# One score tile in twenty of a stage exponentiated on VectorE, in a two-layer transformer kernel; narrow units transposed on TensorE; half-width buffers for tanh-GELU

## The chip, the cores and the metric

The kernel runs on one core of a Trainium2 chip. A core has a matrix engine (TensorE, PE in the profile; its weight loads are PEld), a vector engine (VectorE, DVE), an activation engine (ScalarE, ACT), a general engine (GpSimd, POOL) and a queue that issues transfers (SyncE, SP). They run at the same time, each through its own list of instructions in a fixed order, and wait for each other by semaphores. The metric is the device time of one launch in microseconds (us). Four runs of the kernel before took 1085.89, 1086.05, 1086.89 and 1088.29 us, a median of 1086.47.

## The reference

The input is 2048 rows of 448 numbers in bf16. Two identical layers are applied, each an attention block (A) with 16 heads of 28 and a mixer with an MLP (B):

```python
def _A_ref(x, wqkv, wo):
    B, S, D = x.shape
    H = 16
    Dh = D // H
    qkv = (lambda x, *d: x.transpose(*d))((x @ wqkv).reshape(B, S, 3, H, Dh), 2, 0, 3, 1, 4)
    q, k, v = qkv[0], qkv[1], qkv[2]
    scores = jnp.einsum("bhqd,bhkd->bhqk", q, k) * (Dh ** -0.5)
    p = _softmax(scores, axis=-1)
    o = jnp.einsum("bhqk,bhkd->bhqd", p, v)
    return (lambda x, *d: x.transpose(*d))(o, 0, 2, 1, 3).reshape(B, S, D) @ wo

def _B_ref(x, w1, w2, w3, w4):
    ...
    h = _gelu(_layernorm(x, axis=-1) @ w1)
    ...
    hs = jnp.concatenate([g0, g1, g2, g3], axis=-1) @ w2
    x1 = x + hs
    h2 = _gelu(_layernorm(x1, axis=-1) @ w3) @ w4
    return x1 + h2

x = A_x
x = x + _A_ref(_layernorm(x, axis=-1), A_wqkv, A_wo)
x = x + _B_ref(_layernorm(x, axis=-1), B_w1, B_w2, B_w3, B_w4)
x = x + _A_ref(_layernorm(x, axis=-1), A_wqkv, A_wo)
x = x + _B_ref(_layernorm(x, axis=-1), B_w1, B_w2, B_w3, B_w4)
```

Here g0 to g3 are four column blocks of h, shifted by one or two rows up or down, and gelu is the tanh form.

## The kernel before, in words

**Tiles.** The 2048 rows are 16 tiles of 128. Queries are worked in units of four tiles (512 queries); in the second layer (the code's L = 1) the last four tiles are two narrow units of two tiles. The heads are four groups of four, g = 0 to 3, each head padded from 28 to 32 rows, so that four heads fill the 128 rows of the array. The "middle query units" of the first layer (the code's L = 0) are units 1 and 2.

**Attention.** A segment is one unit, one group of heads and a range of key tiles (all 16, or a part for the units that start before all keys exist; a part's unfinished sum is spilled to DRAM from `u_sb` and loaded again into `uin`). Within a segment, every pair of a key tile and a head is a score tile: 128 keys by 512 queries, one PSUM bank. Score tiles are gathered in granules of three and two by turns, 823 granules for 2048 score tiles. Granule n uses banks 0 to 2 or 3 and 4 (`gbank`). For each, PE computes the scores (`st_ops`), ACT exponentiates the whole granule in one instruction into `PT`, which holds six granules, and PE multiplies it with the values into bank 5 (`t_pv`). The scores of granule n+2 are asked for when the exponentiation of n has been placed, since they use the same banks. At the end of a segment `t_norm` takes the sum out of bank 5, adds the earlier part, and divides by the row of sums. There is no running maximum: a bound, taken from norms of queries and keys, rides along as an extra row of `qT` and keeps the exponent in range.

**The rest.** `kq_proj`, `k_proj`, `q_proj` and `v_proj` make keys, queries and values; `t_outproj` the output projection; `t_mixA` the norm and the matmul with w1, whose gelu `tanh_gelu` computes on VectorE with one tanh on ACT; `t_x1` the matmul with w2 and the second norm; `t_mixB` the MLP, with its hidden rows in `h2T`. `t_gelu` applies the MLP's gelu in batches, since each needs another function table on ACT. Units of one tile at the very end work `direct`: ACT applies gelu as it reads PSUM, and the normalized rows are transposed on PE instead of by a DMA (`transposes`, `pe_transpose`).

**What sets the order.** All this is written as small tasks, generators that yield operations with an estimated duration, the keys they read and write, waits for named events and requests for named resources (banks, buffers). At build time the scheduler `Sched` places one operation after another on the engine lists, by the earliest start and by a rank. It plans twice, each time taking the latest starts of the last plan as the due times of the next, and the final round perturbs the due times at given clock values with given random seeds (`MOVES`). So an edit of one task can move instructions of all the others. Semaphores follow from the keys. While PE would idle, the scheduler places filler matmuls on `ones_bf` into a free bank (the line of the profile with `ones_bf` and 128x256). A lone matmul of four column blocks may be cut into four narrow ones beside the attention products (`cols4`), which is why one operation has two lines in the profile.

Lines of the profile that the prediction uses: L1183 exponentiation; L1157 scores; L1207 products with the values; L1223, L1225 and L1229 the end of a segment; L1294 to L1302 `tanh_gelu`; L1511 batched gelu; L643 and L646 other matmuls, whole and in four; L1547 filler; L909 and L914 the copies of queries and keys on ACT; L918 `sq`; L1473 the copies of the MLP's hidden rows out of PSUM.

Of the kernel before, what the change touches and what calls it, by code (L numbers as in the profile page):

```python
# [496 lines left out]
def build_kernel(nc, A_x, A_wqkv, A_wo, B_x, B_w1, B_w2, B_w3, B_w4, out, n_layers=2):  # L497
# [9 lines left out]
    WSH = 60.0 / SCALE  # L507
# [6 lines left out]
            (0.00, 729633), (12.02, 924040), (24.04, 434439), (36.20, 574974), (48.20, 998734), (60.31, 612851), (84.52, 842410), (96.68, 918064),  # L514
            (108.85, 164590), (120.87, 267692), (157.65, 500181), (169.69, 831239), (181.82, 304948), (230.86, 623460), (267.82, 635046), (279.92, 554061),
            (291.98, 583939), (316.31, 70253), (354.68, 913365), (427.30, 772407), (439.37, 109773), (451.37, 312812), (463.53, 356989), (499.73, 313895),
            (511.74, 819503), (523.90, 509392), (536.08, 765633), (560.47, 911140), (572.67, 320651), (584.70, 124158), (596.84, 268927), (608.90, 282420),
            (623.07, 286925), (647.19, 306544), (671.29, 953155), (683.47, 435091), (720.44, 443516), (732.70, 487532), (744.73, 525952), (756.74, 580821),
            (780.78, 167669), (804.93, 534508), (817.06, 491945), (829.27, 156654), (841.43, 565799), (865.63, 783778), (883.33, 193326), (907.37, 77659),
            (919.44, 633974), (931.74, 778092), (955.90, 220356), (967.93, 984671), (979.95, 491738), (1004.15, 124983), (1016.21, 872429), (1029.60, 388275),  # L520
            (1041.62, 163375), (1053.71, 7157),
# [15 lines left out]
        [([0, 1, 2], 0, 0), ([3, 4, 5, 6], 4, 0), ([7, 8, 9, 10], 0, 1), ([11, 12], 4, 2), ([13, 14, 15], 0, 2)],  # L537
        [([0, 1, 2], 4, 0), ([3, 4, 5, 6], 0, 0), ([7, 8, 9, 10], 4, 1), ([11, 12], 0, 1), ([13], 2, None), ([14, 15], 4, None)],
# [28 lines left out]
    with st:  # L567
# [7 lines left out]
        hot = sb("hot", [128, 4], FP32)  # L575
        ident = sb("ident", [128, 128], BF16)
# [7 lines left out]
        h2T = sb("h2T", [128, 14, 1024], BF16)  # L584
# [32 lines left out]
        PT = sb("PT", [128, 15, 512], BF16)  # L617
        u_sb = sb("u_sb", [128, 512], FP32)
# [478 lines left out]
        def e_dur(n):  # L1097
            return 0.066 + 0.427 * len(grans[n]) if n >= 0 else 0.0
# [18 lines left out]
        def t_uload(si):  # L1117
            L, u, g, p, kts, first, last = segs[si]
            yield ("wait", ("spill", L, u, p - 1, g))
            if not segs[si - 1][5]:  # L1120
                yield ("wait", ("ucopied", si - 1))
# [515 lines left out]
```

## Time and profile before

| | |
|---|---|
| median of four runs | 1086.47 us |
| the profiled execution | 1087.08 us |
| its span, first to last instruction | 1085.4 us |
| PE busy, filler included | 1047.0 us |
| ACT busy | 1036.4 us |
| DVE busy | 597.0 us |
| POOL busy | 54.1 us |
| mean granted TensorE clock | 0.995 |
| moved by DMA | 38.33 MB |

A line of the groups names the line of the code, the engine, the operation, what it writes and reads, the number of instructions, then their busy time in us and the mean of one in ns, and last how long the engine stood idle before them and which instruction ended most of that. Windows give each engine's busy time in a stretch of the span. Durations of neighbouring instructions on one engine can overlap a little, so their sum is somewhat more than the time they take together. Busy time of PE is modelled from pipelined matmuls.

### The profile page before, as it was taken

Reading aid. Unit: us, or ns where it says so; the run is one execution under the profiler, and the core shown is the slowest. Engines: PE = TensorE matmul, PEld = TensorE weight load, DVE = VectorE, ACT = ScalarE, POOL = GpSimd, SP = SyncE. Lnnn points to the kernel's source line nnn. Section 1 sums busy time; section 2 is a strip of 40 time slices with the busy share of each in tenths; the row PEclk is TensorE's granted clock in tenths of the full one; section 3 lists DMA queues with packets and bytes.
Section 4 is the critical chain, followed back from the end, with each engine's and each line's share of the span. In section 5 each row is a group of like instructions: output and inputs, shape, how many; then the busy total and the mean of one; then the engine's idle time right before and its main releaser. Section 6 shows DMA issues by size and latency. Waiting matters only on the chain.

```text
span 1085.4 us, 21565 instructions
## 1 busy us (share of the span) xinstructions
PE 1047.0 (96%) x9390; PEld 409.7 (38%) x9408; DVE 597.0 (55%) x1410; ACT 1036.4 (95%) x938; POOL 54.1 (5%) x76
## 2 busy tenths in 40 slices
PE   8999999999999999999999999999999999999998
PEld 5333333333333432334333333333333333444545
DVE  6976248420573356832688438356957323757434
ACT  4899999999999999999999999999999999999973
POOL 1100000000010000100001000000000000010000
PEclk8999999999999999999999999999999999999999
DMA  4222080000000020000111112214200001000000
GB/s 113 59 84 64 20 193 21 15 1 21 20 21 2 1 40 21 1 21 1 40 40 33 31 31 59 69 30 118 54 20 2 21 10 32 22 21 12 11 18 22
DMA packets 76439, 38.33 MB, mean 35 GB/s; under 512 B 61176, under 2 KB 69752, under 8 KB 76344
## 3 DMA queue, kind: packets, MB, share of 16 engines
q1 hardware_dynamic: 76344, 36.96, 13.3%
q8 instruction: 73, 1.20, 0.5%
q14 instruction: 22, 0.18, 0.1%
HBM read 13.75 MB, written 8.13 MB: 20 GB/s over the span
## 4 chain that ended last, share of the span: by engine, by line
ACT 60%; PE 34%; DVE 5%; DMA 1%; issue 0%; SPq 0%; DVEq 0%; ACTq 0%
ACT PT L1183 53%; PE ps L643 12%; PE ps L1157 8%; PE ps L1207 7%; ACT h2T L1511 4%; PE ps L646 4%; PE ps L1547 2%; ACT gt L1299 1%; DMA xT<-xn 1%; ACT L1511 1%; DMA h2T<-in_A_wqkv_dram 1%; ACT L1183 0%; DVE kT L911 0%; DVE st L805 0%; DVE hT L1290 0%
## 5 line engine op out<-in xcount | busy, mean ns | idle before, releaser
L1183 ACT ACTIVATE PT<-ps 128x1536 bf16<-128x1536 f32 (+1 forms) x823 | 938.3, 1246 | 8.0 <-PE ps L1157 5.4
L1157 PE MATMUL ps<-qT,kT 32*128 32x512 bf16 (+1 forms) x2304 | 320.0, 360 | 14.3 <-ACT PT L1183 7.9
L1207 PE MATMUL ps<-PT,vaug 128*32 128x512 bf16 (+1 forms) x2304 | 249.8, 362 | 3.3 <-ACT PT L1183 1.4
L1547 PE MATMUL ps<-ones_bf 128*128 128x256 bf16 x1234 | 185.5, 278 | 2.6 <-DVE hot L677 1.1
L1157 PEld LDWEIGHTS ps<-qT,kT 32*128 32x128 bf16 x2304 | 80.3, 91 | 264.1 <-ACT PT L1183 155.4
L1473 DVE CAST h2T<-ps 128x512 bf16<-128x512 f32 (+2 forms) x126 | 73.8, 586 | 111.5 <-PE ps L643 88.7
L1547 PEld LDWEIGHTS ps<-ones_bf 128*128 128x128 bf16 x1234 | 102.7, 99 | 85.7 <-issue 62.8
L643 PE MATMUL ps<-xT,w 112*128 112x512 bf16 (+6 forms) x632 | 127.8, 323 | 0.8 <-ACT h2T L1470 0.4
L1207 PEld LDWEIGHTS ps<-PT,vaug 128*32 128x32 bf16 x2304 | 63.4, 94 | 124.1 <-issue 69.3
L643 PEld LDWEIGHTS ps<-xT,w 112*128 112x128 bf16 (+1 forms) x632 | 50.5, 104 | 52.6 <-issue 29.6
L643 PE MATMUL ps<-w,h2T 128*128 128x448 bf16 x259 | 62.2, 362 | 4.0 <-ACT h2T L1511 4.0
L646 PE MATMUL ps<-w,h2T 128*32 128x448 bf16 x756 | 48.7, 353 | 4.4 <-ACT h2T L1511 4.4
L1229 DVE SCALAR_TENSOR_TENSOR u_sb<-uin,fct,ps 128x512 f32<-128x512 f32 x24 | 17.8, 743 | 59.1 <-PE ps L1207 58.0
L646 PE MATMUL ps<-xT,w 112*32 112x512 bf16 (+3 forms) x576 | 48.8, 349 | 0.1
L1490 DVE TENSOR_TENSOR uin<-x_res,ps 128x448 bf16<-128x448 bf16 x16 | 9.8, 619 | 66.1 <-PE ps L643 49.8
L1497 DVE TENSOR_TENSOR x_res<-x_res,ps 128x448 bf16<-128x448 bf16 x16 | 9.9, 620 | 64.3 <-PE ps L646 35.3
L1511 ACT ACTIVATE h2T<-h2T 128x7168 bf16<-128x7168 bf16 (+2 forms) x9 | 44.7, 5008 | 0.1
L805 DVE BATCH_NORM_STATS2 st<-x_res 128x6 f32<-128x448 bf16 x64 | 38.9, 615 | 1.7 <-DMA x_res<-in_A_x_dram 0.9
L1334 POOL TENSOR_TENSOR mst<-mst,neghalf 128x4 f32<-128x4 f32 (+2 forms) x10 | 9.0, 895 | 535.8 <-DVE mst L1333 407.9
L911 DVE TENSOR_SCALAR qT<-ps,bcol 128x512 bf16<-128x512 f32 (+1 forms) x24 | 15.6, 650 | 36.4 <-PE ps L643 35.3
L1432 POOL TENSOR_TENSOR mst<-mst,neghalf 128x1 f32<-128x1 f32 x32 | 22.7, 718 | 255.1 <-DVE mst L1430 218.6
L1223 DVE STREAM_TRANSPOSE u_sb<-ps 128x512 f32<-128x512 f32 (+1 forms) x24 | 15.0, 624 | 34.5 <-PE ps L1207 34.5
(139 smaller groups left out, 901.9 us busy)
## 6 DMA issues: line engine op xcount, KB each, us to landing
uscr<-u_sb SPq DMA_DIRECT2D x24, 256.0 KB, 2.1
uin<-uscr SPq DMA_DIRECT2D x24, 256.0 KB, 2.7
w<-in_B_w_dram SPq DMA_DIRECT2D x2, 1568.0 KB, 14.3
out_dram<-uin SPq DMA_DIRECT2D x16, 112.0 KB, 1.7
x_res<-in_A_x_dram SPq DMA_DIRECT2D x3, 448.0 KB, 8.8
h2T<-in_A_wqkv_dram SPq DMA_DIRECT2D x2, 392.0 KB, 6.0
w<-in_B_w_dram SPq DMA_DIRECT2D x2, 392.0 KB, 8.4
xT<-xn SPq DMA_TRANSPOSE x32, 3.7
```

Source lines behind the costliest of these rows:

```text
L643: return e.matmul(out=dst(0, m), lhsT=lhs(0, m), rhs=rhs, start=start, stop=stop)
L646: return [e.matmul(out=dst(a, min(m, a + 32)), lhsT=lhs(a, min(m, a + 32)), rhs=rhs, start=start, stop=stop, tile_position=(0, a)) for a i ...
L805: yield op("dve", 0.55, lambda e: e.bn_stats(out=st6[:, t, :], in_=x_res[:, t, :]), reads=[("x", t)], writes=[("st6", t)])
L911: yield op("dve", 0.06 + c_ps(nw), lambda e, b=b: e.tensor_scalar(out=dst, in0=ps[:, bi(b), 0:nw], scalar1=bias, scalar2=None, op0=ALU.add ...
L1157: yield op("pe", 0.005 if ph == h else 0.012 + W / 2400.0, lambda e, bk=bk, r0=32 * j, g=g, kc=kc, q0=q0, W=W, c0=W * h: e.matmul(out=ps[: ...
L1183: yield op("act", e_dur(n), lambda e, b0=b0, p0=p0, cnt=cnt: e.activation(out=PT[:, p0:p0 + cnt, :], in_=ps[:, b0:b0 + cnt, :], func=ACT.E ...
L1207: yield op("pe", 0.004 + nt * 0.0133, lambda e, j=j, rhs=rhs, vs=vs, i=i: e.matmul(out=ps[32 * j:32 * j + 32, UBK, 0:128 * nt], lhsT=vaug[ ...
L1229: yield op("dve", 0.06 + c_ps(W), lambda e: e.scalar_tensor_tensor(out=u_sb[:, 0:W], in0=uin[:, :], scalar=fct[:, L, p, g:g + 1], in1=ps[: ...
L1432: yield op("pool", 0.57, lambda e, t=t: e.tensor_tensor(out=mst[:, t, R3:R3 + 1], in0=mst[:, t, V3E:V3E + 1], in1=neghalf[:, 0:1], op=ALU. ...
L1473: yield op("dve", c_ps(NW), lambda e, fch=fch, b=b: e.tensor_copy(out=h2T[:, fch, hoff:hoff + NW], in_=ps[:, bi(b), 0:NW]), reads=[("ps", ...
L1511: yield op("act", c_act(14 * NW), lambda e, c0=c0, NW=NW: e.activation(out=h2T[:, :, c0:c0 + NW], in_=h2T[:, :, c0:c0 + NW], func=ACT.Gelu ...
L1547: SC.fill = (0.13, lambda e, b: e.matmul(out=ps[:, bi(b), 0:256], lhsT=ones_bf[:, :], rhs=ones_bf[:, :].unsqueeze(1).to_broadcast([128, 2, ...
```

## The change

One score tile of some granules no longer goes through ACT. `on_dve` picks granules by their number and by the place of their third tile in its segment. For these ACT exponentiates the first two tiles only, and a task `t_dexp` computes the third on VectorE in seven operations: the scores, in units of the exponent of two, are clamped at zero and written as 32-bit integers with 16 fractional bits; from the low half a correction polynomial is made in fp16 (in `gt`, the buffer of the tanh); the sum of the shifted integer and the correction, written as 16-bit integers into a buffer `PTD` of three slots, is the bit pattern of the power of two in bf16. The third score matmul of granule n+2 waits until the first of these operations has read the bank. The products with the values of such a tile are deferred by `DEFER` key tiles in `t_pv`. So that the same scores serve both engines, queries are scaled by `QS` and ACT's exponentiation has scale `LN2` and a constant bias.

Around it: `h2T` has seven tiles instead of eight, with other places in `MIXB`; units of two tiles or fewer are transposed on PE in `t_mixA`, and in the second layer's `t_mixB`; `tanh_gelu` takes halves of its two work buffers where the unit is at most 256 wide; a later part's sum is added in place in `uin` and spilled from there, and the last part's transpose writes `u_sb`; the batched gelu of a narrow tile of the second layer has no margin in its planned start; and `MOVES` is another list.

```diff
-    WSH = 60.0 / SCALE
+    LN2 = math.log(2.0)
+    QS = SCALE / LN2
+    BIAS2 = 127.0
+    WSH = 60.0 / LN2 + BIAS2
+    DEFER = 4
+    EXPC = (0.30457565 * 128, 0.07826797 * 128)
...
-        [([0, 1, 2], 0, 0), ([3, 4, 5, 6], 4, 0), ([7, 8, 9, 10], 0, 1), ([11, 12], 4, 2), ([13, 14, 15], 0, 2)],
-        [([0, 1, 2], 4, 0), ([3, 4, 5, 6], 0, 0), ([7, 8, 9, 10], 4, 1), ([11, 12], 0, 1), ([13], 2, None), ([14, 15], 4, None)],
+        [([0, 1, 2], 0, 0), ([3, 4, 5, 6], 3, 0), ([7, 8, 9, 10], 0, 1), ([11, 12], 4, 2), ([13, 14, 15], 0, 2)],
+        [([0, 1, 2], 4, 0), ([3, 4, 5, 6], 0, 0), ([7, 8, 9, 10], 3, 1), ([11, 12], 0, 1), ([13], 2, None), ([14, 15], 3, None)],
...
+        t32 = sb("t32", [128, 512], mybir.dt.int32)
...
-        h2T = sb("h2T", [128, 14, 1024], BF16)
+        h2T = sb("h2T", [128, 14, 896], BF16)
...
+        PTD = sb("PTD", [128, 3, 512], BF16)
...
-            b2 = yield from kq_proj(xt, g, wq_pad, "wq_pad", qT[:, g, q0:q0 + nw], wk, bias, bkey, nw)
+            b2 = yield from kq_proj(xt, g, wq_pad, "wq_pad", qT[:, g, q0:q0 + nw], wk, bias, bkey, nw, QS)
...
+        def on_dve(n):
+            if len(grans[n]) < 3:
+                return False
+            L, u, g, p, kts, first, last = segs[grans[n][2][0]]
+            return 1 <= grans[n][2][1] <= len(kts) * UNITS[L][u][1] // 4 - 4 and (104 < n < 300 and n % 8 == 0)
+
+        DVL = [n for n in range(len(grans)) if on_dve(n)]
+        DVN = {n: k % 3 for k, n in enumerate(DVL)}
...
+        def t_dexp(n):
+            bk, slot, at = gbank(n) + 2, DVN[n], DVL.index(n)
+            yield ("acq", ["t32"])
+            yield op("dve", 0.06 + c_ps(512), lambda e: e.tensor_scalar(out=t32[:, :], in0=ps[:, bk, :], scalar1=0.0, scalar2=65536.0, op0=ALU.max, op1=ALU.mult),
+                     reads=[("ps", bk)], writes=[("t32",)], last=[("ps", bk)])
+            yield ("sig", ("d1", n))
+            for r in ("gt0", "gt1"):
+                yield ("acq", [r])
+            fx, ex = gt[:, 0:256].bitcast(FP16), gt[:, 256:512].bitcast(FP16)
+            lo = t32[:, :].bitcast(mybir.dt.uint16).rearrange("p (n two) -> p n two", two=2)[:, :, 0]
+            yield op("dve", c_f2b(512), lambda e: e.tensor_scalar(out=fx, in0=lo, scalar1=2.0 ** -16, scalar2=None, op0=ALU.mult), ...
+            yield op("dve", c_b2b(512), lambda e: e.tensor_scalar(out=ex, in0=fx, scalar1=EXPC[1], scalar2=EXPC[0], op0=ALU.mult, op1=ALU.add), ...
+            yield op("dve", c_f2b(512), lambda e: e.tensor_tensor(out=ex, in0=ex, in1=fx, op=ALU.mult), ...
+            yield op("dve", c_b2b(512), lambda e: e.tensor_scalar(out=fx, in0=fx, scalar1=-1.0, scalar2=None, op0=ALU.add), ...
+            yield op("dve", c_f2b(512), lambda e: e.tensor_tensor(out=ex, in0=ex, in1=fx, op=ALU.mult), ...
+            if at >= 3:
+                yield ("wait", ("pvd", DVL[at - 3]))
+            yield op("dve", 0.06 + c_ps(512), lambda e: e.scalar_tensor_tensor(out=PTD[:, slot, :].bitcast(mybir.dt.uint16), in0=t32[:, :], scalar=2.0 ** -9, in1=ex, op0=ALU.mult, op1=ALU.add),
+                     reads=[("t32",), (("gt",), "gt1")], writes=[pt_key(n, 2)])
...
                 for (h, k, si, i, j) in sorted(mms):
+                    if k == 2 and n - 2 in DVN:
+                        yield ("wait", ("d1", n - 2))
...
-                yield op("act", e_dur(n), lambda e, b0=b0, p0=p0, cnt=cnt: e.activation(out=PT[:, p0:p0 + cnt, :], in_=ps[:, b0:b0 + cnt, :], func=ACT.Exp, scale=SCALE),
+                yield op("act", e_dur(n), lambda e, b0=b0, p0=p0, cnt=cnt: e.activation(out=PT[:, p0:p0 + cnt, :], in_=ps[:, b0:b0 + cnt, :], func=ACT.Exp, scale=LN2, bias=-BIAS2 * LN2),
...
+                    now = [h for h in held if h[0] + DEFER <= i * nt // 4]
...
-                yield op("dve", 0.06 + c_ps(W), lambda e: e.scalar_tensor_tensor(out=u_sb[:, 0:W], in0=uin[:, :], scalar=fct[:, L, p, g:g + 1], in1=ps[:, UBK, :],
+                yield op("dve", 0.06 + c_ps(W), lambda e: e.scalar_tensor_tensor(out=uin[:, :], in0=uin[:, :], scalar=fct[:, L, p, g:g + 1], in1=ps[:, UBK, :],
...
+                usrc, uk = (u_sb, ("u",)) if first else (uin, ("uin",))
+                yield op("sp", 0.1, lambda e: e.dma_start(out=uscr[4 * u + g], in_=usrc[:, :]), reads=[uk], writes=[("uscr", u, g)], dma=True, dma_time=3.0)
...
+            if nw <= 256:
+                r = yield ("acq", ["gw0", "gw1"])
+                held = [r]
...
-            yield from transposes(xs, xt, n, direct)
+            yield from transposes(xs, xt, n, direct or n <= 2)
...
-            yield from transposes(xs, xt, n, direct)
+            yield from transposes(xs, xt, n, direct or (L == n_layers - 1 and n <= 2))
...
-                         reads=allk, writes=allk, tab="gelu", margin=0.0 if k else 1.0, glue=k > 0)
+                         reads=allk, writes=allk, tab="gelu", margin=0.0 if k or (L == n_layers - 1 and n <= 2) else 1.0, glue=k > 0)
```

## The prediction

> **What bounds the kernel now.** I read the page first: busy time of the engines and its slices.
>
> ```profile
> PE 1047.0 (96%) x9390; PEld 409.7 (38%) x9408; DVE 597.0 (55%) x1410; ACT 1036.4 (95%) x938; POOL 54.1 (5%) x76
> ...
> DVE  6976248420573356832688438356957323757434
> ACT  4899999999999999999999999999999999999973
> ```
>
> PE and ACT both look full, so a share of busy time does not say which one limits. The groups with shapes kept apart decide it (columns: names, shapes, count, then busy us and mean ns, then idle before and its releaser).
>
> ```profile
> L1183 ACT ACTIVATE PT<-ps 128x1536 bf16<-128x1536 f32 x410 | 599.8, 1463 | 4.2 <-PE ps L1157 2.5 <-PE ps L1207 0.3
> L1183 ACT ACTIVATE PT<-ps 128x1024 bf16<-128x1024 f32 x405 | 420.9, 1039 | 3.8 <-PE ps L1157 2.9 <-PE ps L1207 0.8
> ...
> L1547 PE MATMUL ps<-ones_bf 128*128 128x256 bf16 x1234 | 185.5, 278 | 2.6 <-DVE hot L677 1.1 <-DVE k L1041 1.0 <-ACT qT L909 0.5
> ```
>
> The 823 exponentiations wait for anything only 8.0 us in all (4.2 + 3.8), while 185.5 us of PE is the filler matmul on `ones_bf`, whose result nobody reads. Without it PE is busy 1047.0 - 185.5 = 861.5 us, 79% of the span. ACT is the bound from the first exponentiation to the last; PE has room. The ACT timeline of the stage that the change touches, and then its windows, show it:
>
> ```profile
> 187.50 110.73 ACT L1183 ACTIVATE PT<-ps 128x1536 bf16<-128x1536 f32 x97
> ```
>
> ```profile
> core 0: us, PE busy (x) PEld busy (x) DVE busy (x) ACT busy (x) POOL busy (x), PEclk, DMA share, GB/s
> 160.00:200.00 40.00, 38.73 (x324) 13.96 (x323) 31.44 (x70) 39.73 (x38) 4.55 (x5) 1.00 0.09 20
> 200.00:240.00 40.00, 39.47 (x329) 15.12 (x327) 9.57 (x18) 40.00 (x37) 0.00 (x0) 1.00 0.02 5
> 240.00:280.00 40.00, 39.12 (x304) 14.95 (x304) 11.63 (x23) 39.94 (x36) 0.00 (x0) 1.00 0.06 14
> 280.00:320.00 40.00, 38.37 (x308) 13.78 (x308) 27.37 (x65) 39.97 (x39) 3.63 (x4) 1.00 0.06 15
> 320.00:360.00 40.00, 38.45 (x341) 14.14 (x345) 14.00 (x25) 39.96 (x32) 1.58 (x2) 1.00 0.06 14
> ```
>
> 97 exponentiations stand back to back for 110.73 us; DVE is 24% to 79% busy meanwhile. The chain of work that ended last agrees: ACT has 60% of it, 53% on the exponentiations' line, and PE's 34% lies in the first 30 us, in the last 37 us and in short steps between two exponentiations.
>
> **The change part by part.**
>
> *The tiles that leave ScalarE.* `on_dve` takes granules 112 to 296 in steps of 8: 24. It drops the six (128, 152, 176, 200, 256, 280) whose third tile lies on a segment's first or last three key tiles. 18 are left. In each, ACT does 128x1024 in place of 128x1536: 1463 - 1039 = 424 ns. 18 x 0.424 = **7.6 us off ACT**, all in the stage shown. The exponentiation's bias is now a number other than zero, in all 823. No row has such a form. Bounds: nothing, or the step between an Identity on 128x512 without and with a bias column (597 and 688 ns), 91 ns each, 823 x 0.091 = 75 us. I take nothing: the tanh (112x512, 637 ns) has a numeric scale and stands nearer to the 597, and the call passes a number, not a column. The Trainium skill, "ScalarE: Activation LUTs", section "What ACT_TABLE_LOAD costs", draws the same line: immediates for scale and bias are in the base cost, each pointer column adds about 93 ns; by it the term is zero.
>
> *The seven VectorE operations for each.* Priced by nearest rows: from PSUM to `t32` 0.74 (128x512 with a scalar, 746 ns); low halves to fp16 0.42 (`sq` 418), or 0.69 if the strided read goes at the pace of a PSUM copy (690); two scalar operations at 0.29 (`gw` 290); two products at 0.42 (423); the last 0.74 (742). Sum 3.32 us, 18 x 3.32 = 60 us of DVE. It was 101.8 us busy from 160 to 380 us, so 162 of about 212, 76%: room on the average. It is not spread evenly. I summed these durations over the changed kernel's VectorE order, from one `t32` operation to the next, against ACT's time for the granules between (110.73 / 97 = 1.14 us each, plus 0.54 for a tanh): granules 112 to 144 hold 38.2 us of VectorE in 37.3 of ACT, 208 to 264 62.5 in 63.4; between and after them 38% to 70%, but for the last eight granules. So there VectorE is full, within the error of such a sum (neighbouring operations overlap by up to 0.08 us, which makes it smaller).
>
> *The new wait.* The third score matmul of granule n+2 may write its bank only when DVE has read it (`d1`). In PE's order the wait stands right there; the attention matmuls, projections and the next granule's scores queue behind it, and ACT behind those. Ends: 0, and 18 x 0.75 = 13.5 us, each read held up by one long VectorE operation that nothing hides. Nearest rows: 32 tanhs need VectorE in time just as these do, and wait 1.5 us in all, 0.047 each; 18 of that are 0.85. With the full stretches I take **+1.0**. The deferred product with `PTD` runs four key tiles later, at least 16 tiles or 7 us, against a chain of 3.3 us (some 6 with what is interleaved): 0 taken; late by 1 us each it would be up to 18.
>
> *PE.* 18 lone `PTD` products cost at most a full-width matmul (0.28) in place of 0.12: 2.9 us, under 56.0 us of filler from 140 to 400 us. With that cover gone they would be paid in full. Filler matmuls fall from 1234 to 1136, which is where 7.6 us less of span and more real work come from.
>
> *Narrow units on TensorE.* DMA transposes of 128x8x128 go from 5 to 3; PE gets 16 transposes (94 ns each, 1.5 us), DVE four copies (0.42 each, 1.7 us), mostly beside exponentiations. SP loses two issues. A DMA transpose takes 3.7 us to land, so the units come at most 2 x 3 us earlier, with ACT on other exponentiations: 0, and neither end beyond -1.5 or +1.5. One thing comes later: the four 128-row tanhs of the unit before the last stand at exponentiations 796 to 799, before 787 to 791, and the last gelu batch still follows exponentiation 813. That leaves 14 exponentiations, 16 us, and 6.2 us of the batch's first half, for a chain of some 14 us (56 matmuls of 256, 14 copies at 0.42, the norm): 0, up to +3.
>
> *In-place `uin`.* Same count of VectorE operations, but 12 spills now leave from `uin`, and the next load waits on SP for the spill to land. A DMA transpose in SP's queue then waits too. Spill 2.1, load 2.7, the operation 0.74, latencies: about 6.2 us from one to the next, against 16 tiles of a short segment, 7.3 us: 0, up to 12 x 1 = +12 if loads slow to 4.8.
>
> *The rest.* Half buffers for tanh, `h2T` with seven columns, `mul` in the projections, `LN2`: same instructions, 0 (a half of `h2T` waited for would cost up to 2 us; its users lie 50 exponentiations apart). The gelu margin only moves the planner's due time; both gelus it could concern come second in their batch. The head gains one Square on ACT where ACT idles 2.9 us for PE: 0. The tail after the last score keeps its matmul counts (237 wide, 109 narrow): 0. The new move list can take away at most the 8.0 us of waits that exist, or add as many; I take 0.
>
> **Sum** against the profiled execution, 1087.08 us (span 1085.4 and 1.7 around it, 0.6 over the median of 1086.47): 1087.1 - 7.6 + 1.0 = **1080.5 us**. Next limits then: PE without filler at 80%, DVE at 61%.
>
> A rule that speaks against all this is in the same page of the Trainium skill, section "Rules for kernel authors": ScalarE is the place, and called the only one, for exp. Were VectorE's chain on the path, a tile would cost 3.3 in place of 0.42, 18 x 2.9 = 52 us slower; the windows above, with VectorE at 46% in the stage, make me take the other sum.
>
> **The rivals.**
>
> *1, slower: VectorE becomes the bound in its two full stretches.* 11 of the 18 tiles lie there, ends counted. For it: my count finds no slack. Against it: in before DVE is 79% busy from 160 to 200 us and ACT idles 0.27. If the chain costs 4.5 us in place of 3.3 (strided and integer forms slow), 11 x 1.2 = 13 us fall on ACT: 1087.1 - 7.6 + 1.0 + 13 = 1093.5. It decides from 0.8 us extra per tile on, where 8.8 us are lost, the saving and the 0.2% that a measurement of this kernel tells from no change (2.2 us).
>
> *2, about no change: the bank comes free late.* Each `d1` 0.4 us late at PE: 18 x 0.4 = 7.2 us, 1086.7. For it: DVE executes in order, and operations stand before `d1` that themselves wait for PE. Against it: the read can start as soon as the granule's scores are there, while ACT works on the granule ahead, and is due when ACT is on the granule behind: nearly two exponentiations of 1.04 us, against 0.74.
>
> *3, the change doesn't do what it says: PE bounds this stage, ACT only idles sooner.* Then nothing is gained, 1087. Against it: 56 us of filler in 260, and 8 us of waits.
>
> *4, more than the sum:* the new order also removes 3 of the 8 us of waits: 1077.
>
> **How the numbers follow.** The forecast with rival 4 beside it: 0.77 (1077 to 1084). Rivals 2 and 3: 0.11 (1084 to 1088). Rival 1, with `uin` or the bias: 0.12. Faster takes in the first and 0.02 of the second; same gets 0.09. The range reaches from rival 4 with one more us to rivals 2 and 3: 1076 to 1087, and leaves out rival 1 and a little on either side.
>
> **What would show it.** Right: 18 exponentiations fewer of 128x1536 and more of 128x1024, at unchanged 1463 and 1039 ns; ACT's idle before them still near 8 us, 9 at most; seven new VectorE groups of 18 or 36, sum near 3.3 us a tile; filler below 175 us; SP's loads landed before VectorE wants them. Wrong: PE waiting for `t32` for several us, ACT's waits for score matmuls up by as much between 160 and 380 us; VectorE above 95% there; a mean of the exponentiations near 1550.

## The result and the profile after

The changed kernel takes 1083.54 us in the median (1079.01 to 1092.93) where the kernel before takes 1086.54: a ratio of 0.9975, 95% interval 0.9967 to 0.9983. It is faster by 3.0 us, where the forecast of 1080.5 meant 6.0. The single runs spread over 14 us; those of before over 5. The profiled execution of after took 1082.26 us, its span 1080.5.

First the line of busy time and instructions of each engine from the page of after, then its groups with shapes kept apart (shapes, count, then busy us and mean ns, then idle before and its releasers). VectorE's seven operations are, in the order of the code, L1130, L1137, L1138, L1140, L1141, L1142 and L1145.

```profile
PE 1040.4 (96%) x9655; PEld 407.8 (38%) x9674; DVE 649.3 (60%) x1539; ACT 1028.7 (95%) x939; POOL 54.3 (5%) x76
```

```profile
L1238 ACT ACTIVATE PT<-ps 128x1536 bf16<-128x1536 f32 x392 | 575.8, 1469 | 11.2 <-PE ps L1212 7.9 <-PE ps L1287 2.6
L1238 ACT ACTIVATE PT<-ps 128x1024 bf16<-128x1024 f32 x423 | 438.6, 1045 | 5.4 <-PE ps L1212 4.9 <-PE ps L1287 0.3
...
L1651 PE MATMUL ps<-ones_bf 128*128 128x256 bf16 x1136 | 171.0, 278 | 2.1 <-DVE hot L683 1.1 <-DVE sq L924 0.6 <-DVE u_sb L1311 0.2
...
L649 PE MATMUL ps<-xT,wq_pad 112*128 112x512 bf16 x89 | 27.1, 405 | 2.5 <-DMA xT<-xn 2.0 <-DVE kmaxc L936 0.4
...
L1130 DVE TENSOR_SCALAR t<-ps 128x512 int32<-128x512 f32 x18 | 12.4, 687 | 17.9 <-PE ps L1212 17.9
...
L1145 DVE SCALAR_TENSOR_TENSOR PTD<-t,gt 128x512 uint16<-128x512 int32 x18 | 12.3, 685 | 0.2
...
L1142 DVE TENSOR_TENSOR gt<-gt 128x512 f16<-128x512 f16 x18 | 7.6, 423 | 0.4
...
L1137 DVE TENSOR_SCALAR gt<-t 128x512 f16<-128x512 uint16 x18 | 7.6, 420 | 0.3
L1140 DVE TENSOR_TENSOR gt<-gt 128x512 f16<-128x512 f16 x18 | 7.5, 418 | 0.3
...
L1138 DVE TENSOR_SCALAR gt<-gt 128x512 f16<-128x512 f16 x18 | 5.2, 291 | 0.3
L1141 DVE TENSOR_SCALAR gt<-gt 128x512 f16<-128x512 f16 x18 | 5.2, 291 | 0.4
```

ScalarE lost 1036.4 - 1028.7 = 7.7 us of work, as summed. But its waits before exponentiations are now 11.2 + 5.4 = 16.6 us, from 8.0: 8.6 us more than before, where the forecast had added 1.0. The two lines name PE as their end, and one line of PE names a transfer: the matmul on `xT` and `wq_pad` waited 2.0 us for the DMA transpose. VectorE's operations wait for PE, not the other way round (17.9 us ahead of `t32`, shown as `t`).

Where the waits grew is seen best when the start of the same exponentiation is compared between profiles. The table gives the start of exponentiation n in before, in us, and how much later (+) or earlier (-) it starts in other profiles, worked out from their traces; one profile is one execution. The last two columns are experiments told of below.

| n | before | after | after, run again | weight loads early | before, tiles skipped |
|---|---|---|---|---|---|
| 0 | 30.6 | -3.4 | -2.3 | -2.4 | +1.0 |
| 100 | 146.2 | -3.9 | -2.7 | -2.8 | +0.6 |
| 125 | 176.0 | -1.0 | +2.0 | -4.9 | +0.1 |
| 300 | 392.4 | -6.6 | -3.6 | -10.4 | -2.0 |
| 450 | 577.4 | -1.1 | +3.3 | -5.0 | -2.0 |
| 650 | 817.5 | -0.9 | +3.7 | -4.7 | -1.9 |
| 822 | 1048.3 | -4.4 | +0.2 | -7.0 | -3.0 |
| end of span | 1085.4 | -4.8 | -0.3 | -7.5 | -3.0 |

Two places stand out in after: 2.9 us are lost between 100 and 125, where the first tiles leave ScalarE, and 5.5 between 300 and 450, the end of layer 0 and the start of layer 1. The chain that ended last in after, at the first place (start us, us, what):

```profile
149.39 0.39 PE ps L1212 x2
149.78 0.16 PE ps L1287
149.93 8.35 DMA xT<-xn
158.28 0.05 issue
158.33 0.39 PE ps L649
```

The windows of after there (busy us and instruction count of each engine, then granted clock, DMA share, GB/s):

```profile
core 0: us, PE busy (x) PEld busy (x) DVE busy (x) ACT busy (x) POOL busy (x), PEclk, DMA share, GB/s
155.00:160.00 5.00, 2.96 (x22) 0.84 (x23) 4.64 (x13) 2.97 (x4) 0.26 (x1) 1.00 0.32 73
160.00:165.00 5.00, 5.00 (x24) 1.01 (x22) 1.38 (x3) 3.85 (x4) 0.90 (x1) 0.51 0.00 0
165.00:170.00 5.00, 5.00 (x28) 1.29 (x27) 3.74 (x9) 3.80 (x5) 0.00 (x0) 0.81 0.45 102
170.00:175.00 5.00, 4.47 (x31) 1.54 (x30) 4.97 (x13) 5.00 (x6) 0.39 (x1) 1.00 0.02 4
```

PE stands for 2.05 us until the transpose lands; then its clock is granted at half (6.8 us from 160.1 on, so 0.51 and then a mixture of half and full), and in 15 us ScalarE is busy 10.62 in place of 15. The chain of before, and its transfers from 140 to 166 us (what, issues, KB each, median us to landing), show that the late transpose was there already:

```profile
153.27 0.04 PE ps L1157
153.31 8.47 DMA xT<-xn
161.78 0.04 issue
161.82 0.40 PE ps L646 x4
```

```profile
w<-in_B_w_dram SPq DMA_DIRECT2D x2, 1568.0 KB, 14.3
w<-in_B_w_dram SPq DMA_DIRECT2D x2, 392.0 KB, 8.4
xT<-xn SPq DMA_TRANSPOSE x1, 8.5
```

It was issued behind two loads of 1568 KB (the MLP's weights w3 and w4) and took 8.5 us, where the median of its kind takes 3.7; it landed 3.2 us after the last of the weight loads. In before, PE had other work until it landed, and ScalarE lost 0.27 us; in the new order the matmul that needs it comes sooner.

### The profile page after: what moved, and what is told of

The parts are those of the page before. It is cut to its first block, busy times and chain, and to the rows that moved or that the text cites. A ratio compares the mean times of both kernels' runs of the same rounds, so it can differ in the third digit from the quotient of the medians.

```text
span 1080.5 us, 22215 instructions
## 1 busy us (share of the span) xinstructions
PE 1040.4 (96%) x9655; PEld 407.8 (38%) x9674; DVE 649.3 (60%) x1539; ACT 1028.7 (95%) x939; POOL 54.3 (5%) x76
## 4 chain that ended last, share of the span: by engine, by line
ACT 58%; PE 36%; DVE 4%; DMA 1%; issue 0%; SPq 0%; POOL 0%; DVEq 0%
ACT PT L1238 51%; PE ps L649 11%; PE ps L1212 10%; PE ps L1287 8%; ACT h2T L1615 4%; PE ps L652 4%; PE ps L1651 4%; ACT gt L1401 1%; DMA xT<-xn 1%; ACT L1238 1%; ACT L1615 1%; DMA h2T<-in_A_wqkv_dram 1%; DVE st L811 0%; DVE qT L952 0%; DVE kmaxc L936 0%
## 5 line engine op out<-in xcount | busy, mean ns | idle before, releaser
L1238 ACT ACTIVATE PT<-ps 128x1024 bf16<-128x1024 f32 (+1 forms) x823 | 930.5, 1243 | 16.6 <-PE ps L1212 12.8
L1287 PE MATMUL ps<-PT,vaug 128*32 128x512 bf16 (+1 forms) x2286 | 256.6, 362 | 3.6 <-ACT PT L1238 2.4
L1651 PE MATMUL ps<-ones_bf 128*128 128x256 bf16 x1136 | 171.0, 278 | 2.1 <-DVE hot L683 1.1
L1651 PEld LDWEIGHTS ps<-ones_bf 128*128 128x128 bf16 x1136 | 94.8, 99 | 77.6 <-issue 58.7
L649 PE MATMUL ps<-xT,w 112*128 112x512 bf16 (+6 forms) x535 | 108.6, 323 | 1.2 <-DVE hT L1374 0.3
L652 PE MATMUL ps<-xT,w 112*32 112x512 bf16 (+3 forms) x964 | 73.6, 339 | 0.0
L649 PEld LDWEIGHTS ps<-xT,w 112*128 112x128 bf16 (+1 forms) x535 | 43.1, 105 | 45.1 <-issue 20.9
L649 PE MATMUL ps<-w,h2T 128*128 128x448 bf16 x250 | 58.8, 354 | 1.3 <-ACT h2T L1615 1.3
L1315 DVE SCALAR_TENSOR_TENSOR uin<-uin,fct,ps 128x512 f32<-128x512 f32 x24 | 17.9, 745 | 57.4 <-PE ps L1287 55.2
L652 PEld LDWEIGHTS ps<-xT,w 112*32 112x32 bf16 (+1 forms) x964 | 30.1, 95 | 11.8 <-DVE h2T L1577 1.6
```

What stands on the lines that cost most here:

```text
L649: return e.matmul(out=dst(0, m), lhsT=lhs(0, m), rhs=rhs, start=start, stop=stop)
L652: return [e.matmul(out=dst(a, min(m, a + 32)), lhsT=lhs(a, min(m, a + 32)), rhs=rhs, start=start, stop=stop, tile_position=(0, a)) for a i ...
L1238: yield op("act", e_dur(n), lambda e, b0=b0, p0=p0, cnt=cnt: e.activation(out=PT[:, p0:p0 + cnt, :], in_=ps[:, b0:b0 + cnt, :], func=ACT.E ...
L1287: yield op("pe", nt * 0.054 if item in late else 0.004 + nt * 0.0133, lambda e, j=j, rhs=rhs, vs=vs, i=i: e.matmul(out=ps[32 * j:32 * j + ...
L1315: yield op("dve", 0.06 + c_ps(W), lambda e: e.scalar_tensor_tensor(out=uin[:, :], in0=uin[:, :], scalar=fct[:, L, p, g:g + 1], in1=ps[:, U ...
L1651: SC.fill = (0.13, lambda e, b: e.matmul(out=ps[:, bi(b), 0:256], lhsT=ones_bf[:, :], rhs=ones_bf[:, :].unsqueeze(1).to_broadcast([128, 2, ...
```

## The experiments

All kernels with "weight loads early" have the same edit behind the planned order, which moves two entries of SP's list ahead of the last loads of `uin` of layer 0:

```diff
+        sp = P.ops["sp"]
+        big = [o for o in sp if o.fn.__defaults__ and (o.fn.__defaults__[0] is w3 or o.fn.__defaults__[0] is w4)]
...
+        for o in big:
+            sp.remove(o)
+            P.all.remove(o)
+        k = sp.index(mark) + 1
+        sp[k:k] = big
...
         P.finalize(nc, st)
```

**The late transpose and the clock.** The changed kernel once more, without an edit:

> The changed kernel once more, beside the experiments on one chip. Theory T1 (transfer, then clock): at 158 us PE stands about 2.0 us for the DMA transpose of xT, issued right behind two weight loads; then the granted clock falls to 0.5 to 0.8 for some 8 us and ScalarE's exponentiations wait 4.4 us in all there. It expects this again in the profile, and a time of 1083.5, with single runs between 1079 and 1090 according to the clock. Rival T0 (the gap belongs to the one profiled execution): no gap of over 1 us at 158 us here.

The changed kernel with the weight loads early:

> The changed kernel with the two MLP weight loads (w3, w4) some places earlier in SP's queue, so that no large load is under way when the transpose of xT at about 150 us is issued; every other engine's order is as it was. T1 (transfer, then clock): PE's wait for the transpose at 158 us falls from 2.0 us to under 0.3, granted clock 1.00 from 160 to 170 us, the waits before exponentiations from 16.6 us to about 12, the time by 4.4 us from 1083.5 to 1079. Rival T2 (the dense stage between the layers, 400 to 560 us, takes back what ScalarE saved): the gap at 158 us goes too, but ScalarE arrives sooner at a stage where it must wait for PE anyway; the time falls by at most 1 us, and the waits from 400 to 560 us grow from 7 to about 11.

The late transpose kept, PE's gap filled; the new matmuls write the bank that the waiting matmul is about to write:

```diff
+        late = next(o for o in pe if dt in o.deps.values())   # first matmul that needs that xT
+        for _ in range(14):
+            f = _Op("pe", lambda e: SC.fill[1](e, bank), False)
+            f.deps = {k: d for k, d in late.deps.items() if not d.dma}
+        ...
+        pe[k:k] = more
```

> The changed kernel with 14 filler matmuls of 256 columns in PE's order right before the matmul that waits for the transpose of xT at 158 us (about 1.5 to 2.1 us of PE work); the transfer is as late as before. T1's second half (PE's idling costs the clock): granted clock 0.95 or more from 160 to 170 us, ScalarE waits about 2.0 us in place of 4.4, the time 1081. Rival (the clock falls for another reason, or the clock loss costs nothing): clock from 160 to 170 us again about 0.66, time 1083.5, or 1 us more where the fillers come late.

And the kernel before with its weight loads early:

> The kernel before with the same two weight loads as early. There the transpose of xT was issued 3 us later and PE had other work while it was under way (ScalarE waited 0.27 us). T1: nothing to win, 1086 to 1086.5. Rival (early weight loads help by themselves, whatever the change does): 1 to 4 us faster here too.

Measured on one chip: after again 1085.04 us (1079.18 to 1091.85), weight loads early 1079.79 (1079.62 to 1080.18), gap filled 1083.79 (1081.80 to 1086.06), before with early loads 1086.54; before itself 1086.57. The ratio to before is 0.9997 (0.9977 to 1.0017) for after again, so that on this chip its gain is not clear of noise, and 0.9944 (0.9927 to 0.9962) for the early loads. The same windows of after again, and then of the early loads:

```profile
155.00:160.00 5.00, 2.60 (x26) 0.89 (x19) 4.06 (x10) 3.23 (x4) 0.00 (x0) 1.00 0.53 92
160.00:165.00 5.00, 5.00 (x25) 1.09 (x24) 1.21 (x6) 3.42 (x3) 1.17 (x1) 0.60 0.00 0
165.00:170.00 5.00, 5.00 (x24) 1.07 (x25) 4.02 (x10) 3.11 (x4) 0.00 (x0) 0.50 0.01 2
170.00:175.00 5.00, 4.59 (x30) 1.25 (x31) 3.21 (x6) 4.28 (x5) 0.00 (x0) 0.87 0.46 105
```

```profile
155.00:160.00 5.00, 5.00 (x41) 1.64 (x38) 4.06 (x11) 5.00 (x5) 0.00 (x0) 1.00 0.01 3
160.00:165.00 5.00, 5.00 (x40) 1.42 (x38) 5.00 (x15) 5.00 (x6) 1.17 (x1) 1.00 0.01 2
165.00:170.00 5.00, 4.47 (x33) 1.46 (x34) 4.83 (x10) 5.00 (x6) 0.00 (x0) 1.00 0.46 105
```

With the loads out of the way ScalarE is busy 15.00 of 15 us, the slowest transpose lands in 4.7 us, and the time falls to the forecast. The spread goes too, from 13 us in 12 runs to 0.6 in 6. Against after run again, 6.8 us are won between n = 100 and 125. The filled gap splits this: PE stands for 1.2 us instead of 2.4, the clock stays at 1.00 from 150 to 175 us, and ScalarE still waits 2.7 us, once, for the transfer. In the two profiles of after ScalarE waits 4.4 and 5.9 us from 155 to 172 us; the longest waits, 2.0 and 2.4, are the transfer's, and the other 2.4 and 3.5 us came at half clock; with the gap filled they are gone. That the stand brought the half clock is argued from these three profiles, one execution each. By the medians this run is only 1.3 us faster than after, not the 2.5 expected, which the runs' spread does not separate from nothing; why not more was not followed up.

Over the 12 runs of after again the time goes with the mean granted clock, for instance 1079.18 us at 0.998, 1083.30 and 1084.35 at 0.995, 1088.08 at 0.991, 1091.60 and 1091.85 at 0.986. The trace shows the half clock in stretches of 3.4 us or a multiple, 6.8 us in the first profile of after and 10.2 in the second. "TensorE: Matmul & The Clock Gate" of the Trainium skill, Part 1, says the same of the gate: two states, full and half, set by a free-running window of about 3.4 us, so that one kernel differs from run to run; it names an idle window of that length as the condition, while here stands of 2.05 and 2.4 us, shorter than that, were followed by half clock.

**What the dense stage takes.** Against the kernel before, the early loads still lose 5.4 us between exponentiations 300 and 450. Is that the price of a ScalarE that arrives sooner, or of the order? In the kernel before, ScalarE skips the third tile of the same 18 granules (L1183):

```diff
-  ... cnt=cnt: e.activation(...)
+  ... cnt=cnt - (n in SKIP): e.activation(...)
```

> The kernel before, its order untouched, in which ScalarE leaves out the third tile of the same 18 granules and nobody computes it (the products read what lay there; that part of the computation is left out). ScalarE alone, without VectorE's chain and without the new order. Prediction's step (18 x 0.424 us off ScalarE come through in full): 1086.5 - 7.6 = 1079, waits before exponentiations still about 8 us. Theory T2a (in the dense stage between the layers, 400 to 560 us, PE is at its limit whatever the order, so a ScalarE that comes sooner waits there): 1083 or more, waits of some 5 us more from 400 to 560 us. T2b (those waits come from the changed kernel's own order): as the prediction's step, under 1 us of waits there.

In the changed kernel, weight loads early, ScalarE gets its work back:

```diff
-  in_=ps[:, b0:b0 + cnt, :]
+  in_=ps[:, b0, :].unsqueeze(1).to_broadcast([128, 3, 512]) if n in DVN else ps[:, b0:b0 + cnt, :]
```

> The changed kernel with the early weight loads (1079.8), in which ScalarE again works 1536 columns in the 18 granules (it reads the first tile's bank three times, so the second tile's products are wrong in those granules; VectorE's chain and all orders stay). ScalarE gets its 7.6 us back. If ScalarE bounds the stage: +7.6 us, 1087.4. If T2 holds in the form that the dense stage takes back what ScalarE gains before it: ScalarE comes later, its waits from 400 to 560 us fall from 6.8 us to 2 or less, and the time rises by only 2 to 3 us, to 1082 to 1083.

VectorE's chain is cut short there, `fx[:, 0:2]`, `ex[:, 0:2]` and a plain scale for the last operation:

> The changed kernel with the early weight loads (1079.8), with the five middle VectorE operations of each of the 18 tiles cut to two columns and the last one a plain scale (the correction of the exponential is left out). VectorE loses about 1.3 us for each tile, 24 us in all. Prediction's step (VectorE hidden): no change, 1079.8 within 0.5. Rival 1 of the prediction (VectorE is the bound in its two full stretches): 3 to 10 us faster.

And some of PE's matmuls are left out in the dense stage:

```diff
+        for k, o in reversed(list(enumerate(pe))):
+            ...                       # neither first nor last term of a sum, planned in 396..425 or 498..552
+                if cut % 2 == 0:
+                    pe.remove(o)
```

> The changed kernel with the early weight loads (1079.8), with 60 of the matmuls between 396 and 425 and between 498 and 552 us left out, each the second or third term of a sum (so projections and MLP there are wrong): some 12 us less of PE in 80 us, all orders as they were. T2 (PE has too much work there and ScalarE waits for it): waits before exponentiations from 400 to 560 us fall from 6.8 us to under 2, the time to 1075. Rival (ScalarE waits there for a chain of single results, not for the amount of PE work): waits still over 5 us, time within 1 us of 1079.8.

Measured: tiles skipped in before 1084.11 us (before 1086.25; ratio 0.9983, 0.9973 to 0.9992); ScalarE's work given back 1086.05; short chain 1079.77; matmuls left out 1078.34 (1077.45 to 1078.71).

The short chain changes nothing: VectorE does not bind. ScalarE's work given back costs 6.3 us, most of its 7.6, and the dense stage takes 6.8 us from a ScalarE that comes late as it took 5.4 from one that comes early: it arrives 6.8 us later there than with the early loads alone, so the loss does not come from arriving early. The difference of 1.4 us between the two looks like the clock's: the profile with ScalarE's work given back has 3.4 us at half clock at 506 us, that of the early loads none there, and the two profiles of after differ in the same way (5.5 us lost without such a stretch, 6.9 with one). The matmuls left out brought 1.4 us, not 5, with 4.9 us of waits left of 6.8: the amount of PE work is only part of it.

Skipping in the order of before was the surprise: 2.1 us of 7.6, and no loss in the dense stage (last column of the table: -2.0 at 300, at 450 and at 650). The 5 us are lost on the spot. Start-to-start times, medians over the 18 granules, in us, from the traces:

```
                          granule n (short)   granule n+1
before                         1.35              0.91
before, tiles skipped          0.92              1.24
weight loads early             0.92              0.91
```

Granule n gets shorter by 0.43, and the next one longer by 0.33: PE, working through an order made for the longer granule, has the next scores ready no sooner. The groups of that run show that the waits are hardly booked as such:

```profile
L1185 ACT ACTIVATE PT<-ps 128x1536 bf16<-128x1536 f32 x392 | 573.0, 1462 | 6.2 <-PE ps L1159 4.5 <-PE ps L1209 0.3
L1185 ACT ACTIVATE PT<-ps 128x1024 bf16<-128x1024 f32 x423 | 436.3, 1039 | 3.5 <-PE ps L1159 2.2 <-PE ps L1209 0.8
```

9.7 us of idle time against 8.0 in before. In the changed kernel the order is laid out anew, PE's other work moves away from the short granules, and all 7.6 us arrive (-2.8 at 100, -10.4 at 300). I took the fillers for what stood in the way and left out a third of them, with the tiles skipped:

```diff
+            if 155.0 < done < 395.0 and ... o.fn.__code__.co_freevars == ("fn",):   # a filler nobody waits for
+                cut += 1
+                if cut % 3 == 0:
+                    pe.remove(o)
```

> The kernel before, ScalarE leaving out the third tile of the same 18 granules as in the run that came to 1084.1 (that tile's part of the computation is left out), and PE without 103 of the 324 filler matmuls that stand in its order among granules 128 to 304; nothing else moved. Theory F (the fillers are instructions like others, in a fixed order made for the slower ScalarE: PE must work through them, and that took 5 of the 7.6 us): between the start of exponentiations 100 and 300 now about 7 us are saved in place of 2.6, and the time is 1079 to 1080. Rival (an exponentiation of 1024 columns saves less than 0.42 us, or PE's real work is the limit there): still 2.6 us, 1084.

1083.16 us: 3.2 us saved between exponentiations 100 and 300 in place of 2.6, far from 7. So leaving out a third of the fillers does not give the 5 us back; what leaving out all of them would bring was not tried. The traces say more. From the start of a short exponentiation n to that of n+2, with tiles skipped, PE stands still for 0.007 us in the mean of the 18. In ten of these stretches it runs no filler at all, only real matmuls, and they got 0.15 us shorter in the mean, of the 0.42 taken from ScalarE; the three in which it runs scores and fillers alone got the whole 0.41 shorter. So in more than half of the places it is PE's real matmuls that the old order leaves no room beside.

**What moved into the dense stage.** Counted in PE's list, 98 matmuls with w4 stand ahead of granule 304 in the kernel before; in the changed kernel 64, and 34 behind it. Three runs with the move list of the kernel before were to say whether VectorE's tiles force that. Edits: `on_dve` false for all granules; the list alone; `on_dve` without granules 208 to 264.

> The changed kernel with no tile on VectorE (823 exponentiations as before), laid out anew with the move list of the kernel before, weight loads early: the rest of the change alone. Prediction's terms for the rest (each 0): 1086.5, and ScalarE's waits from 400 to 560 us about as in before, 0.2 us. Theory V (it is VectorE's tiles that, in the planned order, push MLP work of PE behind granule 304, into the dense stage): no 5 us loss between exponentiations 300 and 450, waits there under 2 us; with the earlier head and tail seen in the changed kernel, 1082 to 1085. Rival M (the narrow units and half buffers cost the 5 us): a loss of 4 us or more there, 1087 to 1090.

> The changed kernel, all 18 tiles on VectorE, weight loads early, laid out anew with the move list of the kernel before. In this order, too, 28 of the 98 matmuls with w4 stand behind granule 304 (34 in the changed kernel, none in the kernel before). Theory V: again 4 to 6 us lost between exponentiations 300 and 450, time 1079 to 1083. Rival L (the changed kernel's own move list made the loss): under 2 us lost there, 1076.

> The changed kernel with the 12 tiles outside VectorE's second full stretch alone (none in granules 208 to 264), laid out anew with the move list of the kernel before, weight loads early. VectorE is free for the MLP's copies there, and 9 of the 98 matmuls with w4 stand behind granule 304. Theory V: saving of 12 x 0.424 = 5.1 us before granule 300, a loss of 0 to 2 us after it, time 1077 to 1079: below the 18 tiles' 1079.8. Rival (ScalarE's time decides alone, the loss in the dense stage stays at 5): 1082.

They took 1105.6, 1115.2 and 1104.32 us. None of the expectations holds, and nothing follows for the tiles: the list had been searched for one program, and with it the three others are 18 to 29 us slower than before. The same programs with lists of their own, below, are not. So each program got a list of its own, by one short search for all:

> The kernel before with a move list made by the same short search from an empty list, weight loads early: the base of this set. Theory: 1087 to 1090, since its own list was searched for longer; under 1086 if that list is not special.

> The changed kernel with no tile on VectorE, and a move list of its own, made by a short search of the same length for all four runs of this set (from an empty list; at each 12 us of the plan 16 seeds are tried twice over, the best kept), weight loads early. The rest of the change alone, in an order made for it. Prediction (each of its terms 0): as the kernel before in the same set, within 1 us. Rival (narrow units, half buffers and in-place sums cost time): 2 to 5 us slower than the kernel before in the same set.

> As the run without tiles, but with the 12 tiles outside granules 208 to 264 on VectorE and a move list of its own. Prediction's step (0.424 us for each tile comes through, where the order is made for it): 5.1 us faster than the run without tiles. Theory V (VectorE's tiles push PE work into the dense stage, above all those of granules 208 to 264): 4 to 5 us faster here, since those six are missing.

> As the run without tiles, but with all 18 tiles on VectorE and a move list of its own. In this order all 98 matmuls with w4 stand ahead of granule 304, as in the kernel before. Prediction's step: 7.6 us faster than the run without tiles, and a loss of under 3 us between exponentiations 300 and 450 against the kernel before. Theory V (whatever the order, the tiles cost about 5 us there): only 2 to 4 us faster than the run without tiles, no faster than with 12.

Two more, from other seeds:

> The changed kernel with no tile on VectorE and a second move list, from the same search begun with other seeds; weight loads early. The first list of this kind came to 1088.2. Theory R (the rest of the change costs about 5 us when every order is searched alike): 1087 to 1090, again 4 us or more over the kernel before with a searched list. Rival (the 5 us between the two were luck of one list): 1082 to 1085.

> The kernel before with a second move list from the same search begun with other seeds; weight loads early. The first came to 1083.0, 3.4 us under the kernel before with its own list. Theory R, and that a list is worth some 3 us by itself: 1082 to 1085. Rival (the 1083.0 was luck of one list): 1086 to 1088, and the two runs without tiles are then no slower than this one by more than 2 us.

| order searched for it | us | against before (1086.47, second lists 1086.40) |
|---|---|---|
| kernel before | 1083.04, second list 1084.25 | 0.9968 (0.9956 to 0.9979), 0.9985 (0.9976 to 0.9995) |
| change without tiles | 1088.21, second list 1086.65 | 1.0017 (1.0008 to 1.0025), 1.0007 (0.9997 to 1.0017) |
| with 12 tiles | 1081.81 | 0.9958 (0.9946 to 0.9970) |
| with 18 tiles | 1080.07 | 0.9941 (0.9921 to 0.9961) |

The kernel before came out under 1086, so its own list is not special, and the second list without tiles fell between its two expectations. The 18 tiles bring 8.1 or 6.6 us against the two lists without tiles, 12 tiles 6.4 or 4.8: the prediction's 7.6 and 5.1 lie between, though either has one list alone. With its own list the kernel with 18 tiles has all 98 matmuls with w4 ahead of granule 304 and loses 0.1 us between 300 and 450. ScalarE's waits from 400 to 560 us (total, times, longest), first of after, then of that run:

```profile
ACT PT L1238 <- PE ps L1212: 4.6, 7, 1.3
ACT PT L1238 <- PE ps L1287: 2.2, 1, 2.2
ACT gt L1401 <- DVE gw L1390: 0.3, 1, 0.3
```

```profile
ACT PT L1238 <- PE ps L1212: 1.8, 3, 1.1
ACT gt L1401 <- DVE gw L1390: 0.6, 1, 0.6
```

So the loss in the dense stage belongs to the order of the changed kernel, not to the tiles as such. All six kernels with a list searched for them have the 98 matmuls ahead of granule 304, and none loses over 1.5 us between 300 and 450; that the 34 late matmuls make the loss is argued from this, not shown by itself. The rest of the change alone costs 2.4 to 5.2 us over the kernel before, searched alike, on average 3.8; two lists of one program differ by 1.2 and 1.6, so that it costs something is likely, how much stays open. Which of its edits it is was not tried. And the kernel before gains 2.2 to 3.4 us from another list (the early loads with it bring it nothing by themselves, 1086.54 against 1086.57): as much as the whole change brought over it.

Its best runs are the early loads and the 18 tiles with their own list, 1079.79 and 1080.07 us, 6.4 to 6.8 us below their before and 3 to 4.5 us below before with a new list.

## Why the prediction was right or wrong

- **Tiles off ScalarE, 7.6 us: right.** ScalarE's work fell by 7.7 us, and with the loads early all of it arrives by exponentiation 300. What it did not say is the condition: the order must be made for it. "PE has room" was true on average and false in the granules: in the old order 5 of the 7.6 us are lost in the next granule.
- **Bias constant, 0 (up to 75): right.** Without tiles, the exponentiations with the constant take 1462 and 1038 ns; before, 1463 and 1039. The 1469 and 1045 ns of after come from exponentiation 650 on, where neighbours overlap more; from start to start they take 1.33 and 0.91 us there, as in before.
- **VectorE's chain, 3.32 us a tile: right** at 687 + 420 + 291 + 418 + 291 + 423 + 685 = 3215 ns. That it would be full in two stretches was wrong: by the trace with early loads VectorE was busy 32.9 of 36.3 us from the first operation of granule 112 to that of 144 (the prediction counted 38.2) and 54.3 of 63.1 from 208 to 264 (62.5), and cutting the chain short changed nothing. Rival 1 falls with this.
- **The new wait `d1`, +1.0: too high.** The waits of PE and its weight loads for `t32` come to 1.0 us in the list of who waited for it (0.3 at the `PTD` products, 0.2 and 0.5 at weight loads of scores and of other matmuls), and the scores' 0.2 is all that `d1` can have cost. Rival 2 falls with this. Rival 3 (PE bounds the stage) is wrong for the changed order and, for most of the 18 places, right for the old one.
- **`PTD` products, fillers: right in substance.** Ten of the 18 products hold PE for 0.31 to 0.32 us, a little over the 0.28 allowed, the others for under 0.01; PE still had 171.0 us of filler (under 175).
- **The head, 0: right in substance.** The first exponentiation is 3.4 us earlier in the profile of after, but the clock differs there: 1.00 from 10 to 30 us against 0.83 in before. In the run with the filled gap, with 0.83, it starts at 30.3 us (30.6 before). With 0, 3.4 and 6.8 us at half clock ahead of it (after, after again, gap filled) it starts 3.4, 2.3 and 0.3 us earlier than in before, which has 6.8: the earlier head is the clock's.
- **Narrow units, half buffers, in-place sums, 0 each: probably too low.** Everything but the tiles cost 2.4 to 5.2 us together in orders searched alike; which edit, and how much beyond the 1.2 to 1.6 us between two lists, stays open. `uin` itself waited 2.2 us for its load, once, on VectorE.
- **The failing step** is in "In-place `uin`" and "The rest": "A DMA transpose in SP's queue then waits too", and "The new move list can take away at most the 8.0 us of waits that exist, or add as many; I take 0". The waits rose by 8.6 us, a little over the bound. The transpose that landed late stood in the profile of before with its 8.5 us and its 1568 KB neighbours; I priced all transposes at the 3.7 us of the median and did not ask what PE does while the slow one is under way in the new order. With the loads out of the way that place gives 5.2 us back on one chip (1085.0 to 1079.8), or 3.8 from the 1083.5 of all runs: more than the 3.0 us that separate forecast and result. The half clock that follows it was no term of the sum.
- **The dense stage, 0:** mis-sized as well, by the 5.4 us lost between exponentiations 300 and 450. The sum does not show it, since the early head (2.4 us), and 2.8 us won between exponentiation 650 and the end, make up for it with the loads early. Both are in part the clock's: before has 6.8 us at half clock in the head and 3.4 at 1034 us, ahead of its last exponentiations; the early loads have 3.4 in the head and 3.4 at 821. That 1079.8 then agrees with the 1080.5 is in part this cancelling, and so luck.

## What to carry to other kernels

Before a change of order, list the transfers that take far longer than their kind, and for each the first instruction that needs it: a transfer that costs nothing today is a wait as soon as its consumer comes sooner. Time taken from a bound engine arrived here only where the engine that feeds it could give up work in the same place; averages over the stage, filler included, don't say so. And where orders are searched, compare programs with orders searched alike: a list costs or brings as much here as the change.

## What was not expected of the hardware

- A stand of PE of 2.05 us was followed by 6.8 us at half clock, one of 2.4 us by 10.2, and one of 1.2 us at the same place by none; in the two profiles of after this made 2.4 and 3.5 us of ScalarE's waits. The length of a stand alone does not decide it. Near 500 us PE stands for 1.98 us in every profile of the changed kernel's order: 3.4 us at half clock follow in after run again and with the gap filled, none in after and with the early loads. And with the early loads 3.4 us at half clock follow a stand of 0.95 us at 819 us. What decides stays open here.
- So single runs of one program lie up to 13 us apart, slower with a lower mean granted clock (0.998 to 0.986).
- A DMA transpose issued behind 1568 KB loads on SP took 6.5 to 9.0 us to land in six profiles, against 3.6 with those loads out of the way; in all six it landed 3.2 us after the last load had. In after, SP's issuing instruction itself lasted 4.8 of the 8.35 us, where others last 1.6. "DMA: Bandwidth & Descriptors" of the Trainium skill, section "Queues, rings and completion order", says that each DMA engine takes the descriptors of a ring in order, and SP owns one row of rings; the landings agree with it, but do not show by themselves whether the transfer waited in a ring or at its issue.
